# Stacking queries and keys through scratch rows in HBM, with a cast in the writing DMA and issues pinned to fixed places

## The chip, the cores and the metric

The kernel runs on one core of one Trainium2 chip. The metric is the device time of one execution in microseconds; lower is better. TensorE is called PE, VectorE DVE, ScalarE ACT, GpSimd POOL, and SyncE SP. SP issues most DMAs of this kernel; its queue is shown as SPq.

## The reference, cut to what matters

Two stages follow each other. The first is attention with a mask by hash bucket (4 batches, 8 heads, 768 rows, head size 64), the second a mixture of 8 experts. Only the first is touched.

```python
q_bits = (np.einsum('bhsd,dk->bhsk', q, proj) > 0)      # 6 bits a row
k_bits = (np.einsum('bhsd,dk->bhsk', k, proj) > 0)
mask = q_bucket[:, :, :, None] == k_bucket[:, :, None, :]
scores = np.where(mask, scale * q @ k.T, -1e9)
attn = softmax(scores) @ v
...                                                     # experts: x @ w1, relu, @ w2, weighted sum
```

## The kernel before

The attention works on groups of 4 heads; there are 8 groups. For each group, keys and queries are transposed, and for each of the two a "stack" of 71 partitions is made: 64 rows of the head's values, and 7 rows made of the bits. One matmul over 71 rows then gives scores and mask together. Making the stack moves rows between partitions, and so it is done by DMA.

```python
def fetch(n):                              # loads of group n, all issued by SP
    ...                                    # k, q: [128, 24*64] f32, one DMA each
    for i in range(2):
        t = lv.tile([P, 2, KT * D], F32, tag="v", name="v")
        for h in range(2):
            hh = g * HG + 2 * i + h
            nc.sync.dma_start(out=t[:, h, :],
                              in_=v[b, hh].rearrange("(r m j) d -> m r (j d)", r=R, m=M4))

def prepare(n):                            # a generator, run in steps among the score matmuls of group n-1
    for name in ("k", "q"):
        tr  = wk.tile([P, 2, S], F32, tag="tr", bufs=1)
        t16 = wk.tile([P, 2, S], F16, tag="t16")
        st  = wk.tile([P, HG, S], F16, tag=name + "s", name=name + "s")
        for c in range(2):
            ...
            pin(nc.vector.transpose(o_ap, i_ap))
            nc.gpsimd.tensor_copy(t16[:, c, :], tr[:, c, :])
            for h in range(HG):
                nc.sync.dma_start(out=st[32 * c:32 * (c + 1), h, :], in_=t16[32 * h:32 * (h + 1), c, :])
            yield None
        ...                                # 16 small matmuls -> pr, and bt = the bits, f16
        ds = scr.tile([HG, HG, 8, QT], F16, tag="ds", name="ds")           # scratch in HBM
        nc.sync.dma_start(out=ds.rearrange("j h r t -> (j h r) t"), in_=bt)
        for h in range(HG):
            nc.sync.dma_start(out=st[D:KR, h, :].rearrange("r (j t) -> r j t", j=HG),   # D = 64, KR = 71
                              in_=ds[:, h, 0:NB + 1, :].rearrange("j r t -> r j t"))
        yield None
        d[name] = st
    ...                                    # POOL casts v and sums it

def scores(n, h, kt):
    for i in range(2):
        pin(nc.tensor.matmul(st[:, i, 0:HT], d["k"][0:KR, h, kt * P:(kt + 1) * P],
                             d["q"][0:KR, h, i * HT:(i + 1) * HT], start=True, stop=True))
    ...
```

`pin` keeps an instruction at its place in the program; what isn't pinned may be moved by a scheduler. The weights of the first expert are loaded by POOL DMAs, which the scheduler placed at the start of the kernel.

The softmax here doesn't subtract the row's maximum and nothing guards it: scores larger than these inputs give would overflow.

Of the kernel before, what the change touches and what calls it, by code (L numbers as in the profile page):

```python
# [8 lines left out]
F32 = mybir.dt.float32  # L9
F16 = mybir.dt.float16  # L10
# [4 lines left out]
Alu = mybir.AluOpType  # L15
# [4 lines left out]
def kernel(  # L20
# [11 lines left out]
    nc = tc.nc  # L32
    B, H, S, D = q.shape
    assert (B, H, S, D) == (4, 8, 768, 64)
    NB = proj.shape[1]
    E = moe_w_gate.shape[1]
    F = moe_w1.shape[2]
    P = 128
# [11 lines left out]
    HG = 4  # L50
    NGRP = H // HG
    R = 32
    M = S // R
    KT = S // P
    M4 = P // R
    QT = S // HG
    KR = D + NB + 1
    BIG = 2048.0
# [3 lines left out]
    def pin(ins):  # L62
        tc.keep_in_program_order(ins)
        return ins

    consts = ctx.enter_context(tc.tile_pool(name="consts", bufs=1))
    pb = consts.tile([P, 2, HG, 8], F32)
    proj4 = consts.tile([P, 2, NB], F32)
    for c in range(2):
        nc.sync.dma_start(out=proj4[:, c, :], in_=proj[32 * c:32 * (c + 1), :].unsqueeze(0)  # L70
                          .to_broadcast([HG, 32, NB]))
    nc.vector.memset(pb, 0.0)
    for a in range(HG):
        sl = slice(32 * a, 32 * (a + 1))
        nc.vector.tensor_copy(pb[sl, :, a, 0:NB], proj4[sl])
    wg_sb = consts.tile([P, DO, E], F16)

    row_i = consts.tile([P, 1], I32)
# [15 lines left out]
    for i in range(2):  # L94
        va = consts.tile([P, HG, KT, D + 1], F16, name=f"va{i}")
        nc.gpsimd.memset(va[:, :, :, D:D + 1], 1.0)
        vs = consts.tile([P, HG, D + 1], F16, name=f"vs{i}")
# [13 lines left out]
    def load_w(e, which, pin=False):  # L111
        if which == 1:
            t = wpool.tile([P, DO, F], F16, tag="w1")
            src = moe_w1[e].rearrange("(do di) f -> di do f", di=P)
        else:
            t = wpool.tile([P, FO, DD], F16, tag="w2")
            src = moe_w2[e].rearrange("(fo fi) d -> fi fo d", fi=P)
        ins = nc.gpsimd.dma_start(out=t, in_=src)  # L118
        if pin:
            tc.keep_in_program_order(ins)  # L120
        weights[e, which] = t
# [47 lines left out]
    wk = actx.enter_context(tc.tile_pool(name="wk", bufs=2))  # L169
    scr = actx.enter_context(tc.tile_pool(name="scr", bufs=4, space=bass.MemoryType.DRAM))  # L170
# [4 lines left out]
    groups = [(b, g) for b in range(B) for g in range(NGRP)]  # L175
    nat, grp = {}, {}

    def fetch(n):
        b, g = groups[n]
        for name, src in (("k", k), ("q", q)):  # L180
            t = ld.tile([P, M, D], F32, tag="nat", name=name)
            nc.sync.dma_start(out=t, in_=src[b, g * HG:(g + 1) * HG].rearrange("h (r m) d -> (h r) m d", r=R))
            nat[name, n] = t
        for i in range(2):
            t = lv.tile([P, 2, KT * D], F32, tag="v", name="v")
            for h in range(2):
                hh = g * HG + 2 * i + h
                nc.sync.dma_start(out=t[:, h, :],
                                  in_=v[b, hh].rearrange("(r m j) d -> m r (j d)", r=R, m=M4))
            nat["v", n, i] = t  # L190

    def prepare(n):

        d = grp[n] = {}
        va, vs = vas[n % 2], vss[n % 2]
        for name in ("k", "q"):
            tr = wk.tile([P, 2, S], F32, tag="tr", bufs=1)
            src = nat[name, n]
            t16 = wk.tile([P, 2, S], F16, tag="t16")
            st = wk.tile([P, HG, S], F16, tag=name + "s", name=name + "s")  # L200
            for c in range(2):
                i_ap = src[:, :, 32 * c:32 * (c + 1)]
                o_ap = tr[:, c, :]
                if name == "k":
                    i_ap = i_ap.rearrange("p (m t) d -> p m t d", m=M4)
                    o_ap = o_ap.rearrange("p (t m r) -> p m t r", t=KT, m=M4)
                else:
                    o_ap = o_ap.rearrange("p (m r) -> p m r", r=R)
                pin(nc.vector.transpose(o_ap, i_ap))
                nc.gpsimd.tensor_copy(t16[:, c, :], tr[:, c, :])  # L210
                for h in range(HG):
                    nc.sync.dma_start(out=st[32 * c:32 * (c + 1), h, :], in_=t16[32 * h:32 * (h + 1), c, :])  # L212
                yield None
            pr = ops.tile([P, 512], F32, tag="o", name="pr")
            for c in range(2):
                for j in range(HG):
                    pin(nc.tensor.matmul(pr[32 * j:32 * (j + 1), 0:QT], pb[:, c].rearrange("p a r -> p (a r)"),
                                         tr[:, c, j * QT:(j + 1) * QT], start=(c == 0), stop=(c == 1)))
            bt = wk.tile([P, QT], F16, tag=name + "b", name=name + "b")
            if name == "k":  # L220
                pin(nc.vector.tensor_scalar(bt, pr[:, 0:QT], 0.0, 0.5, op0=Alu.is_gt, op1=Alu.subtract))
                nc.gpsimd.tensor_scalar(bt, bt, BIG, None, op0=Alu.mult)
            else:
                pin(nc.vector.tensor_scalar(bt, pr[:, 0:QT], 0.0, qoff[:, 0:1], op0=Alu.is_gt, op1=Alu.subtract))
            ds = scr.tile([HG, HG, 8, QT], F16, tag="ds", name="ds")
            nc.sync.dma_start(out=ds.rearrange("j h r t -> (j h r) t"), in_=bt)
            for h in range(HG):
                nc.sync.dma_start(out=st[D:KR, h, :].rearrange("r (j t) -> r j t", j=HG),
                                  in_=ds[:, h, 0:NB + 1, :].rearrange("j r t -> r j t"))
            yield None  # L230
            d[name] = st
        for i in range(2):
            nc.gpsimd.tensor_copy(va[:, 2 * i:2 * i + 2, :, 0:D],
                                  nat["v", n, i].rearrange("p h (t d) -> p h t d", d=D))
        v32 = wk.tile([P, HG, 3, D], F32, tag="v32", bufs=1)
        nc.gpsimd.tensor_tensor(v32, va[:, :, 0:3, 0:D], va[:, :, 3:6, 0:D], op=Alu.add)
        nc.gpsimd.tensor_tensor(v32[:, :, 0], v32[:, :, 0], v32[:, :, 1], op=Alu.add)
        nc.gpsimd.tensor_tensor(vs[:, :, 0:D], v32[:, :, 0], v32[:, :, 2], op=Alu.add)
        yield None

    def scores(n, h, kt):
# [74 lines left out]
    def drain(it):  # L316
        for _ in it:
            pass

    fetch(0)  # L320
    drain(prepare(0))
    fetch(1)
    load_w(0, 1, pin=True)
    nc.gpsimd.dma_start(out=wg_sb, in_=moe_w_gate.rearrange("(do di) e -> di do e", di=P))
    load_w(0, 2, pin=True)

    units = [(n, h, kt) for n in range(len(groups)) for h in range(HG) for kt in range(KT)]
    fill = iter(())
# [1 line left out]
    def take(it, budget):  # L330
        got = 0
        while got < budget:
            try:
                c = next(it)
            except StopIteration:
                return got, True
            got += c or 0
        return got, False
# [5 lines left out]
    for u in range(len(units) + 1):  # L344
        if u < len(units):
            n, h, kt = units[u]
            b, g = groups[n]
            i = u % per
            if i == 0:
                prep = prepare(n + 1) if n + 1 < len(groups) else iter(())  # L350
                if n == 4:
                    load_w(1, 1, pin=True)
                if n == 5:
                    load_w(1, 2, pin=True)
            if i == 20:
                drain(prep)
                if n + 2 < len(groups):
                    fetch(n + 2)
            if u + 1 < len(units):
                pts[u + 1] = scores(*units[u + 1])  # L360
        if u > 0:
            values(*units[u - 1], pts.pop(u - 1))
        if u == len(units):
            break
        if i % 2 == 1 and i > 1:
            next(prep, None)
        if u >= 5 and kt == 3 and h % 2 == 0 and u > 5:
            pn, ph = (n, h - 1) if h else (n - 1, HG - 1)
            pb_, pg = groups[pn]
            turn(pb_, pg * 2 + ph // 2)  # L370
            if pg == NGRP - 1 and ph == HG - 1:
                fill = filler(pb_)
                left = 800 + 16 * 650 + 12 * 865
        elif left > 0:
            slots = 2 * per - (u % (2 * per))
            got, end = take(fill, left / slots - 300)
            left = 0 if end else left - got
        if u % (2 * per) == 2 * per - 1:
            drain(fill)
            fill = iter(())  # L380
            left = 0
# [13 lines left out]
    for it in range(ITERS):  # L395
# [16 lines left out]
                                       op0=Alu.mult, op1=Alu.mult)  # L412
# [11 lines left out]
    for b in range(B):  # L424
        v = xT[:, :, b * S:(b + 1) * S].rearrange("p (dh d) (th t) -> p dh th d t", dh=2, th=2)
# [89 lines left out]
    for n in range(len(work) + 1):  # L515
        h = hidden(*work[n]) if n < len(work) else iter(())
        c = combine(*(work[n - 1] if n else (0, B - 1)))
# [34 lines left out]
```

## Time and profile before

| | before |
|---|---|
| median | 887.58 us (3 runs, 886.33 to 888.19) |
| start of the first score matmul | 39.1 us |
| starts of the eight groups | 39.1, 68.5, 97.0, 129.9, 159.4, 190.8, 219.5, 247.7 us |
| from the last group's start to the end | 639.6 us |

The starts of the groups are the times of every 48th `st` matmul in the trace.

The first lines of the page show busy time and, in 40 slices of 22 us, busy tenths. PEclk is the granted TensorE clock in tenths.

```profile
PE 794.9 (90%) x5392; PEld 431.9 (49%) x5392; DVE 440.8 (50%) x787; ACT 392.4 (44%) x691; POOL 143.0 (16%) x138
...
PE   1278689989996899999999999999999999999993
...
PEclk9998799999998989999999999999999999999997
DMA  7533345734100230023003202300230230001222
```

The expert stage is filled by PE. The attention, the first 12 slices or so, is not: there are holes at the start and in slices 3 to 6.

What PE waited for in the attention is in the view of waits (total us, times, longest):

```profile
PE st L245 <- DMA qs<-ds: 46.4, 6, 26.6
```

`qs<-ds` is the load of the query bits, the last step of a stack. So at most 46 us can be won from these waits.

The cost of the stacking on the queue is in the view of the tile `ks` (min/median/max ns of an issue, first and last start):

```profile
L212 SPq DMA_DIRECT2D ks<-t x64: 507/588/5115, 10.4 to 229.1; - x64
L228 SPq DMA_DIRECT2D ks<-ds x32: 272/299/1219, 27.3 to 234.1; - x32
```

One line of the chain of work (start us, us, what) times three value loads, 96 packets of 1536 B on each of 4 DMA engines:

```profile
113.03 8.22 DMA v<-in_v_dram
```

### The profile page before, as it was taken

Reading aid. Unit: us, or ns where it says so; the run is one execution under the profiler, and the core shown is the slowest. Engines: PE = TensorE matmul, PEld = TensorE weight load, DVE = VectorE, ACT = ScalarE, POOL = GpSimd, SP = SyncE. Lnnn points to the kernel's source line nnn. Section 1 sums busy time; section 2 is a strip of 40 time slices with the busy share of each in tenths; the row PEclk is TensorE's granted clock in tenths of the full one; section 3 lists DMA queues with packets and bytes.
Section 4 is the critical chain, followed back from the end, with each engine's and each line's share of the span. In section 5 each row is a group of like instructions: output and inputs, shape, how many; then the busy total and the mean of one; then the engine's idle time right before and its main releaser. Section 6 shows DMA issues by size and latency. Waiting matters only on the chain.

```text
span 887.3 us, 13608 instructions
## 1 busy us (share of the span) xinstructions
PE 794.9 (90%) x5392; PEld 431.9 (49%) x5392; DVE 440.8 (50%) x787; ACT 392.4 (44%) x691; POOL 143.0 (16%) x138
## 2 busy tenths in 40 slices
PE   1278689989996899999999999999999999999993
PEld 0145455655653445555555555555555555555551
DVE  2023345544637855555555555555555555555551
ACT  0167456657663445554333333333333333333330
POOL 2333214322204310031004001200400040000000
PEclk9998799999998989999999999999999999999997
DMA  7533345734100230023003202300230230001222
GB/s 194 144 115 118 105 141 119 181 118 127 45 2 1 47 46 3 1 48 48 1 2 55 40 1 48 48 1 1 48 48 1 43 52 1 1 1 41 80 82 84
DMA packets 33784, 50.61 MB, mean 57 GB/s; under 512 B 8120, under 2 KB 24504, under 8 KB 33720
## 3 DMA queue, kind: packets, MB, share of 16 engines
q0 software_dynamic: 13072, 16.79, 11.9%
q1 hardware_dynamic: 20648, 32.95, 11.6%
q8 instruction: 42, 0.69, 0.3%
q14 instruction: 22, 0.18, 0.1%
HBM read 53.14 MB, written 7.08 MB: 68 GB/s over the span
## 4 chain that ended last, share of the span: by engine, by line
PE 73%; DMA 9%; DVE 7%; SPq 4%; POOL 2%; ACT 2%; issue 1%; POOLq 0%; ACTq 0%; DVEq 0%
PE yp L139 31%; PE a L462 16%; PE d L462 13%; PE st L245 4%; DMA v<-in_v_dram 4%; DVE hT L471 4%; PE yp L309 3%; SPq L212 2%; DMA qs<-ds 2%; PE num L264 2%; DMA ds<-qb 2%; ACT pt L248 2%; PE hp L301 2%; DMA ds<-kb 1%; PE hp L160 1%
## 5 line engine op out<-in xcount | busy, mean ns | idle before, releaser
L139 PE MATMUL yp<-t,hT 128*128 128x512 f16 x1392 | 375.1, 380 | 0.0
L467 ACT COPY u<-a 128x384 f32<-128x384 f32 x336 | 160.7, 478 | 254.6 <-PE a L462 245.3
L471 DVE CUSTOM_DVE_ANT_0 hT<-d,u 128x384 f16<-128x384 f32 x336 | 179.4, 554 | 142.6 <-PE d L462 85.6
L248 ACT ACTIVATE pt<-st 128x768 f16<-128x768 f32 x192 | 149.1, 809 | 120.8 <-PE st L245 120.3
L139 PEld LDWEIGHTS <-hT 128*128 128x128 f16 x1392 | 136.2, 98 | 117.4 <-issue 1.4
L145 DVE SCALAR_TENSOR_TENSOR acc<-yp,p,acc 128x512 f32<-128x512 f32 x168 | 125.9, 749 | 114.4 <-PE yp L139 110.0
L245 PE MATMUL st<-qs,ks 71*128 71x384 f16 x384 | 102.1, 350 | 52.6 <-DMA qs<-ds 46.4
L462 PEld LDWEIGHTS <-t 128*128 128x128 f16 x896 | 87.8, 98 | 78.5 <-issue 11.0
L462 PE MATMUL d<-xd,t 128*128 128x384 f16 x448 | 110.1, 328 | 4.0 <-DVE hT L471 0.2
L462 PE MATMUL a<-xT,s 128*128 128x384 f16 x448 | 110.1, 328 | 0.3 <-ACT u L467 0.3
L462 PEld LDWEIGHTS <-s 128*128 128x128 f16 x672 | 66.0, 99 | 83.5 <-issue 8.9
L497 ACT ACTIVATE hT<-a 128x384 f16<-128x384 f32 x112 | 54.9, 490 | 75.4 <-PE a L462 74.8
L264 PEld LDWEIGHTS <-pt 128*128 128x128 f16 x1152 | 65.1, 102 | 30.4 <-issue 7.8
L245 PEld LDWEIGHTS <-ks 71*128 71x128 f16 x384 | 34.9, 102 | 75.5 <-issue 40.3
L264 PE MATMUL num<-va,pt 128*128 128x65 f16 x1152 | 70.5, 200 | 0.0
L118 POOL DMA_DIRECT2D t<-in_moe_w_dram x16 | 13.7, 859 | 334.4 <-PE d L462 291.0
L462 PE MATMUL a<-xd,s 128*128 128x384 f16 x224 | 55.0, 328 | 0.0
L462 PE MATMUL a<-xT,t 128*128 128x384 f16 x224 | 54.9, 326 | 0.0
L462 PE MATMUL d<-xT,t 128*128 128x384 f16 x224 | 54.8, 327 | 0.0
L301 PE MATMUL hp<-xT,t 128*128 128x384 f16 x192 | 39.1, 326 | 0.0
L309 PE MATMUL yp<-t,hT 128*128 128x512 f16 x144 | 39.1, 396 | 0.0
L304 DVE TENSOR_SCALAR hT<-hp 128x384 f16<-128x384 f32 x48 | 26.4, 551 | 19.6 <-PE hp L301 19.6
(69 smaller groups left out, 395.6 us busy)
## 6 DMA issues: line engine op xcount, KB each, us to landing
t<-in_moe_w_dram POOLq DMA_DIRECT2D x16, 1024.0 KB, 8.7
k<-in_k_dram SPq DMA_DIRECT2D x8, 768.0 KB
q<-in_q_dram SPq DMA_DIRECT2D x8, 768.0 KB
v<-in_v_dram SPq DMA_DIRECT2D x32, 192.0 KB
out_dram<-acc SPq DMA_DIRECT2D x24, 256.0 KB
ks<-t SPq DMA_DIRECT2D x64, 48.0 KB
qs<-t SPq DMA_DIRECT2D x64, 48.0 KB
ks<-ds SPq DMA_DIRECT2D x32, 10.5 KB
```

The source lines that it names most:

```text
L139: yield nc.tensor.matmul(yp, hT[:, fo, j * P:(j + 1) * P], w2[:, fo, :], start=(fo == 0), stop=(fo == FO - 1))
L145: nc.vector.scalar_tensor_tensor(out=acc[:, blk, :], in0=yp, scalar=pw[:, blk, e:e + 1], in1=acc[:, blk, :], op0=Alu.mult, op1=Alu.add)
L245: pin(nc.tensor.matmul(st[:, i, 0:HT], d["k"][0:KR, h, kt * P:(kt + 1) * P], d["q"][0:KR, h, i * HT:(i + 1) * HT], start=True, stop=True))
L248: pin(nc.scalar.activation(out=pt, in_=st[:, :, 0:HT], func=Act.Exp, scale=scale))
L264: pin(nc.tensor.matmul(num[:, j * (D + 1):(j + 1) * (D + 1)], pf[:, j * P:(j + 1) * P], va[:, h, kt, :], start=False, stop=(kt == KT - 1), ...
L301: pin(nc.tensor.matmul(hp[:, 0:HT], w1[:, do, fo * P:(fo + 1) * P], xT[:, do, b * S + t * HT:b * S + (t + 1) * HT], start=(do == 0), stop= ...
L304: pin(nc.vector.tensor_scalar(hT[:, fo, t * HT:(t + 1) * HT], hp[:, 0:HT], 0.0, None, op0=Alu.max))
L309: pin(nc.tensor.matmul(yp, hT[:, fo, j * P:(j + 1) * P], w2[:, fo, :], start=(fo == 0), stop=(fo == FO - 1)))
L462: yield nc.tensor.matmul(bk, wq[wn][:, do, f * P:(f + 1) * P], xq[xn][:, do, :], start=first and do == 0, stop=do == 1, skip_group_check=True)
L467: nc.scalar.copy(t, bk)
L471: add(TENSOR_ADD_SAT, out=dst, in0=bk, in1=u, s0=3e38, s1=0.0)
L497: nc.scalar.activation(out=hT[:, f, hi], in_=a, func=Act.Relu)
```

## The change

It is meant to make the stack with few DMAs and without casts on POOL: the transposed f32 rows are written to scratch rows in HBM by a DMA that casts, the bits are written beneath them, and one load brings the 71 rows. The Trainium skill ("DMA: Bandwidth & Descriptors", "SWDGE vs HWDGE vs iDMA") ties a cast in a DMA to GpSimd's queue, and so these writes are POOL's. Besides, loads, casts and issues are pinned, and the weights' loads move from the start into the groups.

```diff
@@ prepare
-            tr = wk.tile([P, 2, S], F32, tag="tr", bufs=1)
+            tr = wk.tile([P, 2, S], F32, tag="tr")
             src = nat[name, n]
-            t16 = wk.tile([P, 2, S], F16, tag="t16")
             st = wk.tile([P, HG, S], F16, tag=name + "s", name=name + "s")
+            ds = scr.tile([HG, KR + 1, S], F16, tag="ds", name="ds")
...
-                nc.gpsimd.tensor_copy(t16[:, c, :], tr[:, c, :])
-                for h in range(HG):
-                    nc.sync.dma_start(out=st[32 * c:32 * (c + 1), h, :], in_=t16[32 * h:32 * (h + 1), c, :])
-                yield None
+                if c == 0:
+                    yield None
+            for c in range(2):
+                pin(nc.gpsimd.dma_start(out=ds[:, 32 * c:32 * (c + 1), :], in_=tr[:, c, :]))
+            if n == 0 and name == "q":
+                fetch(0, "v")
+            yield None
...
-            ds = scr.tile([HG, HG, 8, QT], F16, tag="ds", name="ds")
-            nc.sync.dma_start(out=ds.rearrange("j h r t -> (j h r) t"), in_=bt)
-            for h in range(HG):
-                nc.sync.dma_start(out=st[D:KR, h, :].rearrange("r (j t) -> r j t", j=HG),
-                                  in_=ds[:, h, 0:NB + 1, :].rearrange("j r t -> r j t"))
+            eng = nc.scalar if n == 0 and name == "q" else nc.sync
+            for j in range(HG):
+                pin(eng.dma_start(out=ds[:, D:D + 8, j * QT:(j + 1) * QT], in_=bt[32 * j:32 * (j + 1), :]))
+            pin(eng.dma_start(out=st[0:KR], in_=ds[:, 0:KR, :].rearrange("h r t -> r h t")))
...
@@ fetch: pinned; group 0's values by POOL, group 1's k and q by ACT, the rest by SP
@@ main loop: prepare steps at even units, drained at unit 15 (was odd, 20)
+                if n == 0:
+                    load_w(0, 1, pin=True)
+                    ...
+                if n == 1:
+                    load_w(0, 2, pin=True)
+                if n in (4, 5):
+                    load_w(1, n - 3, pin=True)
```

More of the change, by code (lines that the diff above doesn't have):

```diff
@@ L68, with load_proj @@
     proj4 = consts.tile([P, 2, NB], F32)
-    for c in range(2):
-        nc.sync.dma_start(out=proj4[:, c, :], in_=proj[32 * c:32 * (c + 1), :].unsqueeze(0)
-                          .to_broadcast([HG, 32, NB]))
-    nc.vector.memset(pb, 0.0)
-    for a in range(HG):
-        sl = slice(32 * a, 32 * (a + 1))
-        nc.vector.tensor_copy(pb[sl, :, a, 0:NB], proj4[sl])
+    def load_proj():
+        for c in range(2):
+            pin(nc.sync.dma_start(out=proj4[:, c, :], in_=proj[32 * c:32 * (c + 1), :].unsqueeze(0)
+                                  .to_broadcast([HG, 32, NB])))
+        nc.vector.memset(pb, 0.0)
+        for a in range(HG):
+            sl = slice(32 * a, 32 * (a + 1))
+            nc.vector.tensor_copy(pb[sl, :, a, 0:NB], proj4[sl])
     wg_sb = consts.tile([P, DO, E], F16)
@@ L176, with fetch @@
     nat, grp = {}, {}
-    def fetch(n):
+    def fetch(n, what="kqv"):
         b, g = groups[n]
         for name, src in (("k", k), ("q", q)):
+            if name not in what:
+                continue
+            eng = nc.scalar if n == 1 else nc.sync
             t = ld.tile([P, M, D], F32, tag="nat", name=name)
-            nc.sync.dma_start(out=t, in_=src[b, g * HG:(g + 1) * HG].rearrange("h (r m) d -> (h r) m d", r=R))
+            pin(eng.dma_start(out=t, in_=src[b, g * HG:(g + 1) * HG].rearrange("h (r m) d -> (h r) m d", r=R)))
             nat[name, n] = t
-        for i in range(2):
+        for i in range(2 if "v" in what else 0):
             t = lv.tile([P, 2, KT * D], F32, tag="v", name="v")
@@ L187, in fetch @@
                 hh = g * HG + 2 * i + h
-                nc.sync.dma_start(out=t[:, h, :],
-                                  in_=v[b, hh].rearrange("(r m j) d -> m r (j d)", r=R, m=M4))
+                pin((nc.gpsimd if n == 0 else nc.sync).dma_start(
+                    out=t[:, h, :], in_=v[b, hh].rearrange("(r m j) d -> m r (j d)", r=R, m=M4)))
             nat["v", n, i] = t
@@ L209, in prepare @@
                 pin(nc.vector.transpose(o_ap, i_ap))
-                nc.gpsimd.tensor_copy(t16[:, c, :], tr[:, c, :])
-                for h in range(HG):
-                    nc.sync.dma_start(out=st[32 * c:32 * (c + 1), h, :], in_=t16[32 * h:32 * (h + 1), c, :])
-                yield None
+                if c == 0:
+                    yield None
+            for c in range(2):
+                pin(nc.gpsimd.dma_start(out=ds[:, 32 * c:32 * (c + 1), :], in_=tr[:, c, :]))
+            if n == 0 and name == "q":
+                fetch(0, "v")
+            yield None
             pr = ops.tile([P, 512], F32, tag="o", name="pr")
@@ L221, in prepare @@
                 pin(nc.vector.tensor_scalar(bt, pr[:, 0:QT], 0.0, 0.5, op0=Alu.is_gt, op1=Alu.subtract))
-                nc.gpsimd.tensor_scalar(bt, bt, BIG, None, op0=Alu.mult)
+                pin(nc.gpsimd.tensor_scalar(bt, bt, BIG, None, op0=Alu.mult))
             else:
                 pin(nc.vector.tensor_scalar(bt, pr[:, 0:QT], 0.0, qoff[:, 0:1], op0=Alu.is_gt, op1=Alu.subtract))
-            ds = scr.tile([HG, HG, 8, QT], F16, tag="ds", name="ds")
-            nc.sync.dma_start(out=ds.rearrange("j h r t -> (j h r) t"), in_=bt)
-            for h in range(HG):
-                nc.sync.dma_start(out=st[D:KR, h, :].rearrange("r (j t) -> r j t", j=HG),
-                                  in_=ds[:, h, 0:NB + 1, :].rearrange("j r t -> r j t"))
+            eng = nc.scalar if n == 0 and name == "q" else nc.sync
+            for j in range(HG):
+                pin(eng.dma_start(out=ds[:, D:D + 8, j * QT:(j + 1) * QT], in_=bt[32 * j:32 * (j + 1), :]))
+            pin(eng.dma_start(out=st[0:KR], in_=ds[:, 0:KR, :].rearrange("h r t -> r h t")))
             yield None
@@ L232, in prepare @@
         for i in range(2):
-            nc.gpsimd.tensor_copy(va[:, 2 * i:2 * i + 2, :, 0:D],
-                                  nat["v", n, i].rearrange("p h (t d) -> p h t d", d=D))
+            pin(nc.gpsimd.tensor_copy(va[:, 2 * i:2 * i + 2, :, 0:D],
+                                      nat["v", n, i].rearrange("p h (t d) -> p h t d", d=D)))
         v32 = wk.tile([P, HG, 3, D], F32, tag="v32", bufs=1)
-        nc.gpsimd.tensor_tensor(v32, va[:, :, 0:3, 0:D], va[:, :, 3:6, 0:D], op=Alu.add)
-        nc.gpsimd.tensor_tensor(v32[:, :, 0], v32[:, :, 0], v32[:, :, 1], op=Alu.add)
-        nc.gpsimd.tensor_tensor(vs[:, :, 0:D], v32[:, :, 0], v32[:, :, 2], op=Alu.add)
+        pin(nc.gpsimd.tensor_tensor(v32, va[:, :, 0:3, 0:D], va[:, :, 3:6, 0:D], op=Alu.add))
+        pin(nc.gpsimd.tensor_tensor(v32[:, :, 0], v32[:, :, 0], v32[:, :, 1], op=Alu.add))
+        pin(nc.gpsimd.tensor_tensor(vs[:, :, 0:D], v32[:, :, 0], v32[:, :, 2], op=Alu.add))
         yield None
@@ L318, in drain @@
             pass
-    fetch(0)
+    load_proj()
+    fetch(0, 'kq')
     drain(prepare(0))
     fetch(1)
-    load_w(0, 1, pin=True)
-    nc.gpsimd.dma_start(out=wg_sb, in_=moe_w_gate.rearrange("(do di) e -> di do e", di=P))
-    load_w(0, 2, pin=True)
     units = [(n, h, kt) for n in range(len(groups)) for h in range(HG) for kt in range(KT)]
@@ L350 @@
                 prep = prepare(n + 1) if n + 1 < len(groups) else iter(())
-                if n == 4:
-                    load_w(1, 1, pin=True)
-                if n == 5:
-                    load_w(1, 2, pin=True)
-            if i == 20:
-                drain(prep)
+            if i == 15:
+                drain(prep)
+                if n == 0:
+                    load_w(0, 1, pin=True)
+                    pin(nc.gpsimd.dma_start(out=wg_sb, in_=moe_w_gate.rearrange("(do di) e -> di do e", di=P)))
+                if n == 1:
+                    load_w(0, 2, pin=True)
+                if n in (4, 5):
+                    load_w(1, n - 3, pin=True)
                 if n + 2 < len(groups):
@@ L364 @@
             break
-        if i % 2 == 1 and i > 1:
+        if i % 2 == 0:
             next(prep, None)
```

## The prediction

> What bounds the kernel now. The page gives PE 795 of 887 us, so the expert stage (from about 320 us) is bound by TensorE and the diff leaves it alone. The attention is not: by the list of `st` matmuls its eight head groups start at 39.1, 68.5, 97.0, 129.9, 159.4, 190.8, 219.5 and 247.7 us, some 30 us each; 639.6 us follow the last start. The view of waits has PE idle 46.4 us in six waits for `qs<-ds`, 26.6 of it before the first score. The change aims at those.
>
> Removed: 32 POOL casts (0.8 us each), 128 stacking DMAs of 48 KB on 16 engines (0.59 us of SP issue each) and 64 small loads. The weights leave the start. Were the replacement free, I would expect some 40 us less: about 845 us.
>
> Added: per stack two casting DMAs from GpSimd, four writes of bits, and ONE load of 71 partitions x 4 x 1536 B (436 KB). The Trainium skill ("DMA: Bandwidth & Descriptors", "Why a DMA increments its semaphore by 16 and not by 1") says that a hardware-queue DMA uses the largest number of engines up to 16 that divides the slowest dimension of both sides. This trace agrees: each `ks<-ds` load of 7 partitions leaves 7 completion packets of 4 B, each `v` load (slowest dimension 4) 4, and with 16 for the others the count up to 280 us is 3144, as the trace has it. 71 is prime: one engine, 284 packets in series.
>
> Cost. Three `v` loads on 4 engines (96 packets of 1536 B per engine) took 8.2 us in the chain of waits, some 72 ns a packet. So a 71-row load takes about 20.5 us plus about 3 us of issue and completion (an estimate from these numbers), and k and q share that engine. The q bits also have a share on engine 0 in the same queue behind the k load, so the q load cannot be issued before the k load has passed. Per group, estimated: fetch of k, q, v ahead on engine 0 13.5 us, bits and completion 3.5, k load 20.5, bits and completion 3.5, q load 20.5: about 61 us, against 30 us of compute that hides under it. The four weight loads in the attention add about 6 us each on that engine. The prelude's two loads share the engine: first score at about 58 us.
>
> Sum: 58 + 3 x 61 + 4 x 67 = 509 us for the start of the last group, + 640 = 1150 us. All of the added time is on the critical path.
>
> Prediction: 1150 us, 8 in 10 between 1040 and 1240. Faster by over 2%: 4%; within 2%: 3%; slower by over 2%: 93%.
>
> Shown right by: one completion packet and about 284 x 70 ns between first and last packet for `ks<-ds` and `qs<-ds`; group starts some 60 us apart; PE idle 200 to 270 us before `st`, released by DMA `qs<-ds`; PE about half busy in the attention; from the last group's start to the end again about 640 us.
>
> Wrong if: the load is spread over engines (then about 845 us, the first score near 20 us); packets on a lone engine run nearer 50 or 100 ns (about 1070 or 1270 us); the q load overlaps the fetches otherwise than I have it (10 us per group).

## More of the kernel before

The view by windows, cut at the first score and at the start of the last group, gives busy microseconds of each engine in each stretch:

```profile
core 0: us, PE busy (x) PEld busy (x) DVE busy (x) ACT busy (x) POOL busy (x), PEclk, DMA share, GB/s
0.00:39.00 39.00, 3.45 (x32) 0.91 (x33) 7.58 (x17) 1.28 (x1) 13.77 (x28) 1.00 0.71 179
39.00:248.00 209.00, 183.98 (x2028) 116.96 (x2028) 88.59 (x167) 131.35 (x171) 59.24 (x70) 0.93 0.40 116
248.00:887.00 639.00, 607.45 (x3334) 314.00 (x3331) 344.67 (x603) 259.78 (x519) 69.96 (x40) 0.98 0.16 30
```

## The result, and the profile after

| | before | after |
|---|---|---|
| median | 887.16 us (4 runs) | 1145.8 us (4 runs, 1144.82 to 1148.74) |
| first score | 39.1 us | 67.6 us |
| starts of the groups | 39.1 ... 247.7 us | 67.6, 132.2, 196.7, 256.1, 316.4, 382.2, 447.7, 503.9 us |
| last group's start to the end | 639.6 us | 639.8 us |

The changed kernel is slower by 29%: the ratio is 1.292, 95% interval 1.2892 to 1.2948. All outputs are right. Ratios, here and below, are the mean time of one kernel's fast runs over that of the other's fast runs of the same rounds, and so not quite the ratio of the medians quoted.

The page after, the same lines:

```profile
PE 805.3 (70%) x5392; PEld 436.4 (38%) x5392; DVE 442.3 (39%) x787; ACT 393.7 (34%) x691; POOL 142.6 (12%) x142
...
PE   1051331909091633738899999999999999999995
...
PEclk9996575959586775959899999999999999999998
DMA  5143342323241443200220220220401302200122
```

By windows, cut again at the first score and at the last group's start:

```profile
0.00:67.50 67.50, 3.45 (x32) 0.91 (x33) 5.62 (x15) 1.28 (x1) 12.26 (x27) 1.00 0.38 94
67.50:504.00 436.50, 190.62 (x2027) 120.06 (x2027) 90.79 (x169) 132.00 (x171) 60.27 (x75) 0.71 0.32 71
504.00:1143.00 639.00, 611.27 (x3334) 315.45 (x3333) 345.90 (x603) 260.41 (x519) 70.10 (x40) 0.98 0.16 30
```

PE does the same work in the middle stretch (191 us against 184) but takes 436 us for it in place of 209. The third stretch is the same. The DMA engines are not busy on average: 0.32 of sixteen. And PE's waits:

```profile
PE st L253 <- DMA qs<-ds: 295.9, 8, 55.2
```

One period, from the chain of work (the group that starts at 256.12 waits for its queries):

```profile
227.68 6.58 DMA ds<-qb
234.34 21.65 DMA qs<-ds
256.12 0.80 PE st L253 x2
```

and SP's queue at the same time (start us, us of issuing, what):

```profile
206.79 2.56 SPq L236 DMA_DIRECT2D ds<-kb  x4
213.75 0.26 SPq L237 DMA_DIRECT2D ks<-ds  x1
214.12 14.14 SPq L236 DMA_DIRECT2D ds<-qb  x4
234.34 0.24 SPq L237 DMA_DIRECT2D qs<-ds  x1
234.62 11.99 SPq L188 DMA_DIRECT2D k<-in_k_dram  x1
246.67 0.43 SPq L188 DMA_DIRECT2D q<-in_q_dram  x1
```

The trace also holds the single DMA packets (this table is counted from the packed trace, it is no view of `prof`). Around this keys' load it has, counted by size on the hardware queue of SP:

```
what                          packets   first start   last start   spacing (median)
1536 B, load of keys              284      215.81 us    233.13 us      0.061 us
4 B, completion of it               1      233.19 us
4 B, completions of ds<-qb         12      227.2 to 229.1 us   (3 for each of the four DMAs)
4 B, completions of ds<-qb          4      233.3 to 233.8 us   (the fourth of each)
1536 B, load of queries: first             235.23 us
```

A 4 B packet is read here as a completion: each DMA engine that has a share of a DMA writes one when this share is done, and the counts below fit this. 284 packets (71 rows x 4 heads) go one after the other, 61 ns apart, and one completion packet follows: one DMA engine does it all, 17.3 us. The writes of the query bits run on four engines; three are done at 229 us, and the fourth, which also has the keys' load, delivers only after the last key packet. Then the load of the queries follows on that engine. The queue is held up too: of the 14.14 us for the four writes of query bits, 12.25 are the issue of the first one, just behind the keys' load. Over the attention, the completion packets of hardware queues number 648, which is just 16 loads x 1, plus 16 for each of the 16 loads of k and q, 4 for each of 28 value loads on those queues and of 64 bit writes, and 8 for the two loads of `proj`.

### The profile page after: what moved, and what is told of

It reads as the page before. It is cut to its first block, busy times and chain, and to the rows that moved or that the text cites. A ratio compares the mean times of both kernels' runs of the same rounds, so it can differ in the third digit from the quotient of the medians.

```text
span 1143.7 us, 13468 instructions
## 1 busy us (share of the span) xinstructions
PE 805.3 (70%) x5392; PEld 436.4 (38%) x5392; DVE 442.3 (39%) x787; ACT 393.7 (34%) x691; POOL 142.6 (12%) x142
## 4 chain that ended last, share of the span: by engine, by line
PE 63%; DMA 22%; DVE 6%; SPq 5%; ACT 2%; issue 1%; POOL 0%; ACTq 0%; DVEq 0%
PE yp L142 24%; DMA qs<-ds 16%; PE a L471 12%; PE d L471 10%; PE st L253 6%; SPq L236 5%; DMA ds<-qb 4%; PE yp L317 3%; DVE hT L480 3%; PE hp L309 3%; PE num L272 2%; ACT pt L256 2%; DMA ds<-tr 1%; PE pr L226 1%; PE hp L163 1%
## 5 line engine op out<-in xcount | busy, mean ns | idle before, releaser
L142 PE MATMUL yp<-t,hT 128*128 128x512 f16 x1392 | 374.5, 380 | 0.0
L253 PE MATMUL st<-qs,ks 71*128 71x384 f16 x384 | 106.1, 362 | 302.0 <-DMA qs<-ds 295.9
L272 PEld LDWEIGHTS <-pt 128*128 128x128 f16 x1152 | 67.5, 105 | 33.0 <-issue 11.9
L279 DVE RECIPROCAL rn<-num 128x6 f32<-128x6 f32 x32 | 6.3, 196 | 173.5 <-PE num L272 173.5
L272 PE MATMUL num<-va,pt 128*128 128x65 f16 x1152 | 72.8, 203 | 0.0
L219 POOL DMA_DIRECT2D ds<-tr x32 | 22.6, 705 | 356.0 <-DVE tr L215 352.7
L320 DVE COPY acc<-yp 128x512 f32<-128x512 f32 x18 | 12.5, 692 | 125.0 <-PE yp L317 125.0
L471 PE MATMUL a<-xT,t 128*128 128x384 f16 x224 | 55.2, 328 | 0.0
## 6 DMA issues: line engine op xcount, KB each, us to landing
ds<-tr POOLq DMA_DIRECT2D x32, 192.0 KB, 10.5
out_dram<-acc SPq DMA_DIRECT2D x24, 256.0 KB
```

Source lines behind the costliest of these rows:

```text
L142: yield nc.tensor.matmul(yp, hT[:, fo, j * P:(j + 1) * P], w2[:, fo, :], start=(fo == 0), stop=(fo == FO - 1))
L272: pin(nc.tensor.matmul(num[:, j * (D + 1):(j + 1) * (D + 1)], pf[:, j * P:(j + 1) * P], va[:, h, kt, :], start=False, stop=(kt == KT - 1), ...
L471: yield nc.tensor.matmul(bk, wq[wn][:, do, f * P:(f + 1) * P], xq[xn][:, do, :], start=first and do == 0, stop=do == 1, skip_group_check=True)
```

## The experiments

Theory A: the load of 71 rows runs on one DMA engine, because 71 is prime, and this sets the period. Rival B: the casting writes through HBM (10.5 us from issue to landing in the page after) set it. Rival C: the new fixed order on one queue sets it.

### 72 rows in place of 71

```diff
-            pin(eng.dma_start(out=st[0:KR], in_=ds[:, 0:KR, :].rearrange("h r t -> r h t")))
+            pin(eng.dma_start(out=st[0:KR + 1], in_=ds[:, 0:KR + 1, :].rearrange("h r t -> r h t")))
```

Row 71 was already written to the scratch rows, and no matmul reads it.

> The changed kernel, with each stack's load taking 72 rows (one more, already written, row) in place of 71. Theory A (71 is prime, so the load runs on one DMA engine; 72 = 6 x 12 gives 12): 24 packets per engine in place of 284, a load of about 2 us of packets in place of 17; first score near 32 us, group starts about 29 us apart, total 870 us (850 to 900). Rival B (the casting writes and their 10.5 us to landing hold the groups up): still over 1050 us, since nothing of them changes and one row more is moved. Rival C (the fixed order of issues on one queue holds the groups up): still over 1050 us, the order is the same.

Measured: 897.19 us (3 runs), ratio to before 1.0092 (1.0039 to 1.0145). One row more to move took away 249 us. The group starts are 33.2, 65.8, 96.5, 126.5, 156.9, 190.6, 225.8 and 256.0 us. Its completion packets outnumber the changed kernel's by 176 (920 against 744 in the whole program), which is 16 loads x 11: each load now ran on 12 engines. A is right; B and C, as causes of the 29%, are not. The total is at the upper end of what was expected, and the view of waits tells why there is more to win:

```profile
PE st L253 <- DMA qs<-ds: 54.1, 6, 20.9
```

### 64 and 7 rows, and 62 and 9 rows

```diff
-            pin(eng.dma_start(out=st[0:KR], in_=ds[:, 0:KR, :].rearrange("h r t -> r h t")))
+            for lo, hi in ((0, 64), (64, KR)):          # the other run: 62
+                pin(eng.dma_start(out=st[lo:hi], in_=ds[:, lo:hi, :].rearrange("h r t -> r h t")))
```

> The changed kernel, with each 71-row load issued as two, of 64 and of 7 rows: the same bytes, one issue more. Theory A: 16 and 7 engines, 16 + 4 packets on the busiest one, total 870 us (850 to 900). Rivals B and C: no gain or a little loss from the additional issue, over 1050 us.

> As the run with 64 and 7 rows, but cut into 62 and 9 rows: same bytes and same number of issues. 62 = 2 x 31 allows only 2 engines. Theory A gives a dose between: 31 x 4 + 4 = 128 packets on the first engine at 61 us per thousand, 7.8 us per load in place of 17.3, so about 19 us less per group than the changed kernel: group starts about 43 us apart, total about 990 us (950 to 1030). Without theory A it is the same as the run with 64 and 7 rows.

Measured: 908.58 us with 64 and 7 (ratio 1.0199), 986.03 us with 62 and 9 (ratio 1.1068). Bytes and number of issues are the same in both, and the sums of rows too. With 62 = 2 x 31 the first engine has 128 packets, and the groups start 37.5 to 46.1 us apart, as estimated (43). So it is a dose: 284, 128 and 20 packets on the busiest engine gave 1146, 986 and 909 us. With 64 and 7 it was 9 us above the upper end of what was expected, and slower than with 72 rows. Nothing was gained from 16 engines over 12; whether the additional issue per stack costs the 11 us was not tested (the view of waits has PE there wait 33.6 us in four waits for a fetch of keys, which the 72-row run does not have).

### The cast back on POOL, the 71-row load kept

```diff
-                pin(nc.gpsimd.dma_start(out=ds[:, 32 * c:32 * (c + 1), :], in_=tr[:, c, :]))
+                pin(nc.gpsimd.tensor_copy(t16[:, c, :], tr[:, c, :]))
+                pin(nc.sync.dma_start(out=ds[:, 32 * c:32 * (c + 1), :], in_=t16[:, c, :]))
```

(`tr` has one buffer here, as in the kernel before.)

> The changed kernel with the 71-row load, but the casting DMAs from GpSimd replaced by the earlier POOL cast and a plain f16 write to the scratch rows from SP (with tr single-buffered as before, to fit). Theory A: the load is what counts, so still 1100 us or more; rather slower than the changed kernel, since the plain writes run on 4 engines of the same queue as the loads, 128 packets a group on the first of them, some 8 us per group: up to 1210 us. Rival B (casting writes): back to 880 to 950 us.

Measured: 1164.64 us, ratio 1.3074. The casting writes aren't what makes it slow; without them it is a little slower, as A said. The rows still go through HBM in this run, as they do in the 72-row run.

### The prime alone, put into the kernel before, and its twin

```diff
-                    nc.sync.dma_start(out=st[32 * c:32 * (c + 1), h, :], in_=t16[32 * h:32 * (h + 1), c, :])
+                    for lo, hi in ((0, 31), (31, 32)):  # the twin: (0, 30), (30, 32)
+                        nc.sync.dma_start(out=st[32 * c + lo:32 * c + hi, h, :],
+                                          in_=t16[32 * h + lo:32 * h + hi, c, :])
```

> The kernel before, with each of its 128 stacking copies of 32 rows issued as two, of 31 rows and of 1 row. Theory A (the largest divisor up to 16 of the row count is the number of engines; 31 is prime): 16 x 31 packets a group on the first engine at some 85 ns, 42 us, where 32 rows had 2 packets on each engine; group starts about 55 us apart, total near 1090 us (1020 to 1150). If what matters is the number of issues on the queue: the same as the twin with 30 and 2 rows.

> The twin control: the kernel before, each stacking copy issued as 30 and 2 rows. The same number of issues and the same bytes as with 31 and 1, but 15 and 2 engines. Theory A: only the additional issues cost, 128 more at about 0.55 us on a queue that is not the limit: 885 to 930 us.

Measured: 1043.98 us with 31 and 1 (ratio 1.175), 977.06 us with 30 and 2 (ratio 1.0997). The difference of 67 us between the twins is the prime's, at the same number of issues and bytes. The total of completion packets does not show it here: up to the last group it is 3272 in both, 17 for each pair of copies. It is 1 + 16 with 31 and 1, where the single row goes as 16 packets of 96 B, and 15 + 2 in the twin. The packets in time do show it. In a period of the 31-row run the trace has about 16 packets of 1536 B per us for 18 us on end, and little less for ten more: one engine's 61 ns again; the 85 ns that I had put in was too high, and so was the total.

The twin was a miss: 977 in place of 885 to 930. 128 more issues were not free. SP's queue in one period of the twin:

```profile
250.00 8.93 SPq L188 DMA_DIRECT2D v<-in_v_dram  x4
260.14 12.54 SPq L213 DMA_DIRECT2D ks<-t  x16
272.79 0.34 SPq L227 DMA_DIRECT2D ds<-kb  x1
273.23 2.44 SPq L213 DMA_DIRECT2D qs<-t  x3
275.78 1.44 SPq L229 DMA_DIRECT2D ks<-ds  x4
277.26 10.03 SPq L213 DMA_DIRECT2D qs<-t  x13
287.40 0.35 SPq L227 DMA_DIRECT2D ds<-qb  x1
287.79 0.43 SPq L182 DMA_DIRECT2D k<-in_k_dram  x1
288.93 1.31 SPq L229 DMA_DIRECT2D qs<-ds  x4
```

From 250 to 290 us the queue issues almost without a break, and one period is 36 to 46 us. Summed from the first group's start to the last, SP issues for 208 of 277 us, where it was 112 of 209 in the kernel before. It reads as if the issuing itself had become the limit; no run takes this apart further. It suggests that the intent of the change, fewer issues, was a sound one.

### The query bits and the queries' load on ACT's queue in every group

```diff
-            eng = nc.scalar if n == 0 and name == "q" else nc.sync
+            eng = nc.scalar if name == "q" else nc.sync
```

> The changed kernel with the 71-row loads, but the bits and the load of the queries issued from ACT's queue in every group, not only in the first: they no longer stand in one queue behind the keys' load. Theory A (all of it is throughput of one DMA engine): the bits land at once, but both loads now share the engine and still need 568 packets x 61 ns = 35 us a group, with fetches and value loads some 50 us: group starts 52 to 60 us apart in place of 62, total 1060 to 1130 us. Theory C (the order on one queue is what costs): the two loads overlap fully, about 20 us less per group: under 1010 us.

Measured: 1187.89 us, ratio 1.3362: outside both expectations, and as a test of A against C inconclusive. The wait that I meant to take away was replaced by another, and ACT, which also computes the exponentials, had to stand still for it:

```profile
245.05 0.22 ACTq L237 DMA_DIRECT2D qs<-ds  x1
245.37 1.51 ACT L256 ACTIVATE pt<-st 128x768 f16<-128x768 f32 x2 [25.57 <-DMA k<-in_k_dram]
```

The bits landed at 228 us, but the queries' load was issued at 245, just after a fetch of keys had completed, whose share on the first engine stood behind the 71-row load in SP's queue. The load seems to wait for a completion semaphore that the fetch uses too; this is not shown. Nor is it so in every group: the view of ACT's waits has two that end with a fetch of keys (57.4 us), and five that end with the casting writes (53.0 us). What a free order would bring with the prime kept was thus not measured; it doesn't matter, since the 72-row run kept the order.

### Better forms: scratch rows for 16 engines, and the value loads too

In the 72-row run the casting write took 10.8 us from issue to landing. Its destination's slowest dimension is the 4 heads, so it has 4 engines. The scratch is laid out anew, so that a write is 128 contiguous rows:

```diff
-            ds = scr.tile([HG, KR + 1, S], F16, tag="ds", name="ds")
+            ds = scr.tile([2, HG, 32, S], F16, tag="ds", name="ds")
+            db = scr.tile([HG, HG, 8, QT], F16, tag="db", name="db")
...
-                pin(nc.gpsimd.dma_start(out=ds[:, 32 * c:32 * (c + 1), :], in_=tr[:, c, :]))
+                pin(nc.gpsimd.dma_start(out=ds[c].rearrange("h r t -> (h r) t"), in_=tr[:, c, :]))
...
+            pin(eng.dma_start(out=db.rearrange("j h r t -> (j h r) t"), in_=bt))
+            for c in range(2):
+                pin(eng.dma_start(out=st[32 * c:32 * (c + 1)], in_=ds[c].rearrange("h r t -> r h t")))
+            for h in range(HG):                         # the bits, as in the kernel before
+                pin(eng.dma_start(out=st[D:KR, h, :].rearrange("r (j t) -> r j t", j=HG),
+                                  in_=db[:, h, 0:NB + 1, :].rearrange("j r t -> r j t")))
```

> A better form of the changed kernel: the scratch rows laid out so that a casting write is 128 contiguous rows (16 engines in place of 4), the load issued as 32, 32 and 7 rows (16, 16 and 7 engines), the bits through their own scratch by one write and four loads as in the kernel before. Theory: with the prime load gone, what held the 72-row run at 30 to 35 us per group is the casting write on 4 engines (10.8 us from issue to landing); on 16 engines it should land in 4 to 6 us, the waits for the stacked queries vanish except the first, group starts 28 to 29 us apart, first score at 25 to 30 us: total 865 us (850 to 885), so 2 to 3% faster than the kernel before. If the writes' landing is all fixed cost (issue, receipt), no gain over the 72-row run's 897.

Measured: 861.06 us (4 runs), ratio 0.9677 (0.9645 to 0.9708). The DMA issues (last number: median us from issue to landing) of the 72-row run and of this one:

```profile
ds<-tr POOLq DMA_DIRECT2D x32, 192.0 KB, 10.8
```

```profile
ds<-tr POOLq DMA_DIRECT2D x32, 192.0 KB, 4.8
```

From the fourth group on, the groups start 27.3 to 27.9 us apart, and two waits for the queries are left:

```profile
PE st L257 <- DMA qs<-db: 17.4, 2, 11.1
```

This run also cuts the load and gives the bits their own scratch, so that the 36 us against the 72-row run are those of three edits, and not of the writes alone.

Then the value loads, whose slowest dimension is 4 as well, are issued per block of 32 rows, two heads in one:

```diff
-            for h in range(2):
-                hh = g * HG + 2 * i + h
-                pin((nc.gpsimd if n == 0 else nc.sync).dma_start(
-                    out=t[:, h, :], in_=v[b, hh].rearrange("(r m j) d -> m r (j d)", r=R, m=M4)))
+            hh = g * HG + 2 * i
+            for m in range(M4):
+                pin((nc.gpsimd if n == 0 else nc.sync).dma_start(
+                    out=t[R * m:R * (m + 1)],
+                    in_=v[b, hh:hh + 2].rearrange("h (r m j) d -> m r h (j d)", r=R, m=M4)[m]))
```

> As the run with the scratch rows for 16 engines, and also the value loads issued per block of 32 rows, two heads in one, on 16 engines in place of 4 (8 DMAs a group in place of 4). Theory: values land sooner after their fetch and the first four engines are no longer busier than the others; a small gain, most of it in the start (values of the first group, 16 us from issue to landing in the 72-row run, hold POOL's pinned order up): 855 us (840 to 880).

Measured: 849.36 us (4 runs, 848.01 to 850.91), ratio 0.956 (0.9539 to 0.9581): the best version, 39 us better than the kernel before in the same rounds (888.78 us). By windows, cut at its first score and its last group's start:

```profile
0.00:22.00 22.00, 3.68 (x33) 0.95 (x34) 5.63 (x15) 0.00 (x0) 10.05 (x28) 1.00 0.70 188
22.00:208.00 186.00, 175.03 (x2025) 113.08 (x2024) 90.66 (x169) 131.80 (x172) 59.37 (x79) 0.98 0.73 179
208.00:847.00 639.00, 608.28 (x3337) 314.45 (x3334) 344.14 (x603) 260.23 (x520) 70.15 (x40) 0.98 0.16 30
```

Against before, the prelude is 17 us shorter and the middle stretch 23 us. PE is busy for 175 of its 186 us. The DMA share has gone up to 0.73 without holding PE up. How much of this is the stacking's? The value loads alone, in the kernel before:

> The kernel before with the value loads alone changed as in the best run (per block of 32 rows, 16 engines in place of 4, 8 DMAs a group in place of 4); stacking as before. It tells how much of the best run's gain has nothing to do with the stacking. If the stacking through scratch rows is worth most of it: 875 us (865 to 888), about 1% better than the kernel before, from the start. If the value loads were what held the kernel before: 850 to 860 us, as the best run.

Measured: 874.08 us (4 runs, 868.1 to 878.5), ratio 0.9849 (0.9813 to 0.9884). So about a third of the gain, if the two parts add up, has nothing to do with the stacking.

## Why the prediction was right

- **What decides.** The prediction named the 71-row load, on one engine, from the quoted rule and from the 7-row loads of the trace before. The trace after has the one completion packet and 284 packets in series; one row more takes 249 us away, and the prime put into the kernel before costs 67 us over its twin.
- **Size of a load.** Estimated 20.5 us at 72 ns a packet; measured 17.3 us at 61 ns for the keys. The packets of a lone engine run closer together than I took from the value loads. (Their 8.22 us over 96 packets would be 86 ns; 72 takes off 1.3 us for the start, which the prediction doesn't say.)
- **The period.** Estimated 61 us, 67 with a weight load. Measured 56.2 to 60.3, and 64.5 to 65.8 in the four groups with a weight load. Cut at the issues of the loads, the parts are: from a group's start to the keys' load 16.5 to 18.9 us (estimated 17.0), from there to the queries' load 20.2 to 20.6, or 26.2 to 27.6 with a weight load (estimated 24 and 30), and from there to the next group's start 19.4 to 21.8 (estimated 20.5). So most of the error lies in the keys' load. In the first part the casting writes, which I had left out, are what the keys' load waits for last in three of the seven groups, 7.7 us in all; in the other four it waits last for the bits, so their share is small.
- **The order.** "The q load cannot be issued before the k load has passed" is just what the packets show: the fourth completion of the bit writes comes at 233.3 us, after the last key packet at 233.13.
- **The prelude.** Estimated 58 us, measured 67.6: the mis-sized term. The casting writes of the first queries landed only at 28.5 us, with the values' loads in the same queue, and both loads of the stacks began later than estimated: 58 us less two loads of 20.5 leaves 17 us, and they were issued at 24.1 and 28.5 us.
- **A sign that missed.** PE's waits for the queries were to be 200 to 270 us and are 295.9. Without the first, 55.2 us before the first score, they are 240.7.
- **The rest.** Start of the last group estimated 509 us, measured 503.9; the remainder 640, measured 639.8; the total 1150, measured 1145.8. The good agreement of the total is in part luck, with +9.6 us in the prelude and -15 us over the seven periods.
- **Not realized.** The gain that the change aimed at, "about 845 us" were the replacement free, is nearly there: with the loads and writes spread over the engines it is 861.06 us, and 849.36 us with the value loads as well, which are no part of the change.

## What to carry to other kernels

Before one DMA is put in place of many, look at the slowest dimension of both of its sides: in every case here the largest divisor up to 16 was the number of engines, and a prime such as 71 or 31, or a small count such as 4, leaves most engines out. Count completion packets, or compare the time between issue and landing with that of a well-shaped DMA of the same size, since a mean DMA share of a third (0.32 here) hides one engine that everything waits for. One row of padding, or a cut into 64 and 7, can be worth more than the whole idea of the change.

## What the Trainium skill lacked or had wrong

- "DMA: Bandwidth & Descriptors", "Why a DMA increments its semaphore by 16 and not by 1": the rule for the number of engines held in every case here (71 rows: 1 completion; 72 rows: 12; 7 rows: 7; outermost 4: 4). The section gives no cost, but the page's "Specifications" have about 27 GiB/s (29 GB/s) for one engine. Here a 436 KB load on one engine took 17.3 us for its packets, 61 ns for each of 1536 B, which is 25 GB/s.
- The same page, "Rules for kernel authors": it advises to coalesce small transfers into one large one, and not to bother with disjoint partition halves. Here one load of 71 rows against two of 64 and 7 rows was 1145.8 against 908.58 us. The advice needs the condition that the one transfer uses as many engines. The same table has it, in another row ("Use all 16 engines"), which asks for a multiple of 16 as the outermost dimension.
- The same page, "Issuing engines are not separate DMA queues": it calls the time that a sequencer takes to issue usually small relative to the DMA. With 128 more issues (30 and 2 rows) the kernel took 977.06 in place of 888.78 us, and SP's queue issued for 208 of 277 us. That the issuing was the limit was not tested alone.
- No page has how much longer an issue itself takes when an engine of its queue is behind ("Perfetto Trace Analysis" only draws the descriptor buffer as full). The six fetches of keys on SP behind the 71-row load of queries took 11.8 to 12.0 us to issue, and the first write of query bits behind the keys' load 11.8 to 19.3; in the 72-row run, which differs by the one row alone, they took 0.4 to 0.8 and 0.6 us.
- No page has what the GpSimd queue does with a DMA that uses 4 engines: in the changed kernel and in the 72-row run each casting write came with about 384 additional packets of 4 B (it would be 32 for each of the other 12 engines, which is a guess), which the form on 16 engines does not have (12944 against 656 such packets in the attention). That these cost time was not tested alone.
- "TensorE: Matmul & The Clock Gate", "Part 1: The HAM clock gate", agrees: it says that the clock falls to half when PE has been idle. The records after show half the clock for 27 to 48 us in each of the first seven periods, and a granted clock of 0.71 there against 0.93 before. A reader may take this for a cause; but PE's busy time rose by only 10.4 of the 259 us, and the clock of the whole run is 0.875 here and back at 0.961 in the 72-row run.
